# The product of attention's values and factors moves to the end of its period, in front of the split of x

## The chip, the cores and the metric

The kernel runs on one core of one Trainium2 chip. The metric is the device time of one execution in microseconds (us). Engines are named as in the profile: PE (TensorE, matrix products), DVE (VectorE), ACT (ScalarE), POOL (GpSimd) and SP (SyncE, which issues the loads).

## What is computed

Attention with a window of 128 keys and four sink keys, followed by a PReLU network and a mixture of four ReLU experts, all on 1536 tokens of 512 values:

```python
scores = scale * np.matmul(q, k.transpose(0, 1, 3, 2))     # 2 batches, 8 heads, 768 tokens, 64 wide
scores = np.where(is_sink | in_window, scores, -1e9)
a = np.exp(scores - np.max(scores, axis=-1, keepdims=True))
a = a / (np.sum(a, axis=-1, keepdims=True) + 1e-09)
x = np.matmul(a, v)                                         # heads side by side: 1536 x 512
h = x @ w_in                                                # 512 to 2048
x = (np.maximum(h, 0) + alpha * np.minimum(h, 0)) @ w_out   # 2048 to 512
p = domain_probs / (domain_probs.sum(-1, keepdims=True) + 1e-9)
for e in range(4):
    out += p[:, e:e+1] * (np.maximum(x @ w1[e], 0) @ w2[e]) # 512 to 1024 to 512
```

## The kernel before

Each fp32 matrix is split into a high part (rounded to the format that PE multiplies fast) and a low remainder, and a product is three matmuls: high by high, high by low, low by high. Only attention's own products of values and its transposes run on unsplit fp32.

Attention goes through 48 "heads" j of 256 queries (2 batches, 3 blocks of 256 tokens, called units, 8 heads each), one in each **period** p of the loop in `fast`. The work on one head is spread over several periods, so that engines work on different heads at a time. In period p the loop emits, in this order: the split of q and k for head p+2 (`at_split`, ACT); the scores of head p (in periods under 10 of head p+1; `at_scores`, PE); the masking and the row maximum (`at_mask`, DVE, line L587); in odd periods `at_sinks` (PE, L647 and L650); the exponentials (`at_exp`, ACT, L608); in even periods `at_values`, `at_scale` and `at_norm`; the low part of q (`at_split_lo`, DVE, L546); then matmuls of the PReLU network on units that are already through attention (L253 to L255 and L262 to L264), with its PReLU on DVE (`prelu`, L286 and L287) and, where a group of products ends, the copy or addition of its sums (L798, L800); the transposes of the exponentials of head p-1 (`at_turn`, PE L629), and in even periods the split of x (`at_x`: the high part on ACT L698, the low part on POOL L699). At the end, weights are split a piece further (`tick`, L106 to L126). All engines take their instructions in the order in which the program emits them.

Heads are finished in pairs j, j+1 with j even. These are the steps of a pair that matter here:

- period j+2: `at_norm` on DVE makes the reciprocals of the row sums (L617, L618) and copies each to 64 columns (`rw`, L619).
- period j+3: `at_sinks` on PE transposes the sink columns (L647; none for the first unit of a batch) and `rw` (L650) into one PSUM tile `pst`; ACT copies them out (`st` L653, `rb` L655). `rb` are the factors.
- period j+4: `at_values` on PE multiplies values by transposed exponentials into the PSUM tile `pv` (L676); `at_scale` on DVE multiplies `pv` by `rb` into `xf` (L686), the product of this document's title; `at_x` splits `xf`.

So the even period p holds `at_values`, `at_scale` and `at_x` of the pair p-4 and `at_norm` of the pair p-2, and period p+1 holds `at_sinks` of the pair p-2. The tiles `pst` and `pv` share one buffer:

```python
ps = self.psa.tile([P, CH], F32, tag="pv", name=f"pst{j}", bufs=1)   # at_sinks
ps = self.psa.tile([P, CH], F32, tag="pv", name=f"pv{j}", bufs=1)    # at_values
```

The transposes of `at_sinks` in period p+1 can therefore begin only when `at_scale` of period p has read `pv`, and `at_values` of the next pair only when ACT has copied `pst` out. The scores have two buffers. After the 48 heads, `rest` runs the larger part of the PReLU network and the experts.

Of the kernel before, what the change touches and what calls it, by code (L numbers as in the profile page):

```python
# [54 lines left out]
class Body:  # L55
# [661 lines left out]
    def fast(self):  # L717
        nc, tc = self.nc, self.tc
        self.work = accp = tc.alloc_tile_pool(name="accp", bufs=1)
        for c in range(NC):  # L720
            self.acc[c] = accp.tile([P, 4, CH], F32, name=f"acc{c}")
        psb = self.psb = tc.alloc_tile_pool(name="psb", bufs=1, space=PSUM)
        with tc.tile_pool(name="psa", bufs=1, space=PSUM) as self.psa:
            at = self.at = tc.alloc_tile_pool(name="at", bufs=1)
            tmp = tc.alloc_tile_pool(name="tmp", bufs=1)
            self.atk = tc.alloc_tile_pool(name="atk", bufs=1, side="right")
            self.late = []
            for j in range(3, QK):
                self.at_load(j)
            for j in range(2):  # L730
                self.at_split(j)
                self.at_split_lo(j)
            self.plan(*range(EARLY))
            NP, items, before = NU * H, [], None
            for i, visits in enumerate(LEAD):
                steps = [(u, f, f == f0, f == f1 - 1) for u, f0, f1 in visits for f in range(f0, f1)]
                for j, step in enumerate(steps):
                    at_p = LAG + i * H + j * H / len(steps)
                    items.append((at_p, "s1", step))
                    if before:  # L740
                        items.append((at_p + H / len(steps) / 2, "s2", before))
                    before = step
            items.append((NP + 3, "s2", before))
            gs, outs, seen = {}, None, set()
            for p in range(NP + 4):
                if p + 1 >= WHOLE:
                    self.at_load(p + QK + 1)
                self.at_split(p + 2)
                if p in AHEAD:
                    self.busy(psb, 1, f"ahead{p}", tag="h", bufs=2)  # L750
                for j in [0, 1] if p == 0 else [p + 1] if p + 1 < SOON else [] if p < SOON else [p]:
                    self.at_scores(j)
                    if j == 0:
                        self.busy(psb, BETWEEN, "busy", tag="h", bufs=2)
                    if j < WHOLE:
                        self.at_load(j + QK)
                if p > max(LOADS) or p in LOADS:
                    self.load_due(1)
                if FILL.get(p):
                    self.busy(psb, FILL[p], f"busy{p}", tag="h", bufs=2)  # L760
                self.at_mask(p)
                if p == 1:
                    next(self.later_masks)
                if p % 2:
                    self.at_sinks(p - 3)
                self.at_exp(p)
                if p % 2 == 0:
                    self.at_values(p - 4)
                    self.at_scale(p - 4)
                    self.at_norm(p - 2)  # L770
                self.at_split_lo(p + 2)
                if p == 2 * H:
                    self.shares()
                turn = [p - 1]
                while items and items[0][0] < p + 1:
                    _, what, step = items.pop(0)
                    u, f, first, last = step
                    n = slice(u % 2 * UN, (u % 2 + 1) * UN)
                    if what == "s1":
                        ps = psb.tile([P, CH], F32, tag="h", name=f"h{u}_{f}", bufs=2)  # L780
                        self.ready(f)
                        self.s1(f, self.xh[u // 2][:, :, n], self.xl[u // 2][:, :, n], ps[:, :UN])
                        while turn:
                            self.at_turn(turn.pop())
                        gs[step] = self.prelu(tmp, ps[:, :UN], UN, f, f"a{u}_{f}")
                        continue
                    if first:
                        outs = [psb.tile([P, 2, UN], F32, tag="o", name=f"o{u}_{f}_{i}", bufs=2) for i in range(2)]
                    self.s2_transposed(
                        f, *gs.pop(step), [outs[d // 2][:, d % 2, :] for d in range(4)], first, last, [True, False] * 2  # L790
                    )
                    while turn:
                        self.at_turn(turn.pop())
                    if last:
                        for i in range(2):
                            acc = self.acc[u // 2][:, 2 * i:2 * i + 2, n]
                            if u in seen:
                                nc.vector.tensor_tensor(acc, outs[i], acc, ALU.add)  # L798
                            else:
                                nc.vector.tensor_copy(acc, outs[i])  # L800
                        seen.add(u)
                while turn:
                    self.at_turn(turn.pop())
                if p % 2 == 0:
                    self.at_x(p - 4)
                if p == NP + 3:
                    tmp.release()
                    at.release()
                    self.add_late()
                if p < NP + 3:  # L810
                    self.tick(p in STARTS)
                if p == NP - 1:
                    self.atk.release()
                    self.add_late()
                    self.plan(*range(EARLY, SLOTS))
        with tc.tile_pool(name="wide", bufs=1) as wide:
            self.rest(wide, range(len(LEAD), NU), 1)
        psb.release()
        for late in self.late[::-1]:
            late.release()  # L820
        accp.release()
# [232 lines left out]
```

## Time and profile before

| | us |
|---|---|
| median of 3 runs | 896.14 |
| lowest and highest | 894.75, 896.15 |
| the profiled execution, its own time | 895.68 |
| its span in the profile | 893.9 |

The profile is of one execution. Its span runs from the first to the last recorded instruction; what lies around it is 895.68 - 893.9 = 1.78 us. Attention takes the time up to about 207 us, the rest of the networks what follows.

### The profile page before, as it was taken

To read this page: it belongs to the slowest core of one execution; us is meant where nothing else is said; L and a number is where in the kernel's file an instruction comes from. 1 tells how busy PE (TensorE), PEld (TensorE's weight loads), DVE (VectorE), ACT (ScalarE), POOL (GpSimd) and SP (SyncE) were. 2 spreads that over 40 slices of the span, in tenths; PEclk is the share of its full clock that TensorE was granted. 3 is DMA by queue.
4 is the path that set the end of the run, shared out by engine and by line. 5 is a ranking of instruction groups with operands and counts; after the bars stand their busy time and mean duration, and the time that the engine had idled before them with its cause. 6 is when DMAs were issued, how large, how long until landed. Compare 5 with 4: busy or idle time off the path is not lost.

```text
span 893.9 us, 13192 instructions
## 1 busy us (share of the span) xinstructions
PE 881.4 (99%) x4956; PEld 747.4 (84%) x4956; DVE 560.0 (63%) x1104; ACT 330.8 (37%) x773; POOL 368.9 (41%) x349
## 2 busy tenths in 40 slices
PE   9999999999999999999999999999999999999997
PEld 6578899998888888888888888888888888888886
DVE  5778877657995553456655665665566556656654
ACT  4787766754431222233312321231233223212310
POOL 1366644535763454475224404421441344044210
PEclk9999999999999999999999999999999999999999
DMA  5754432302332020000011101101110111011003
GB/s 163 190 184 146 154 120 84 100 1 71 119 118 71 12 70 13 1 25 23 1 48 48 41 7 48 48 3 46 47 48 1 48 48 36 12 48 48 1 1 146
DMA packets 23722, 54.51 MB, mean 61 GB/s; under 512 B 3168, under 2 KB 3168, under 8 KB 23648
## 3 DMA queue, kind: packets, MB, share of 16 engines
q1 hardware_dynamic: 23504, 53.57, 19.0%
q8 instruction: 41, 0.67, 0.3%
q14 instruction: 33, 0.27, 0.1%
q10 hardware_dynamic: 144, 0.00, 0.0%
HBM read 50.42 MB, written 3.15 MB: 60 GB/s over the span
## 4 chain that ended last, share of the span: by engine, by line
PE 93%; DVE 4%; issue 1%; ACT 1%; POOL 0%; DVEq 0%; ACTq 0%; POOLq 0%
PE o L437 9%; PE o L436 9%; PE o L438 9%; PE h L374 5%; PE h L375 5%; PE h L376 5%; PE h L253 5%; PE h L254 5%; PE h L255 5%; PE o L262 5%; PE o L263 5%; PE o L264 5%; PE pv L676 3%; PE c L374 3%; PE c L376 3%; PE c L375 3%
## 5 line engine op out<-in xcount | busy, mean ns | idle before, releaser
L441 DVE SCALAR_TENSOR_TENSOR acc<-o,prob,acc 128x512 f32<-128x512 f32 x180 | 135.1, 751 | 100.3 <-PE o L438 100.3
L140 POOL TENSOR_TENSOR wl<-wraw,wh 128x512 fp32r<-128x512 f32 x60 | 76.6, 1297 | 280.8 <-ACT wh L139 280.8
L437 PE MATMUL o<-wl,hgh 128*128 128x512 f32 x240 | 93.5, 389 | 0.0
L438 PE MATMUL o<-wh,hgl 128*128 128x512 f32 x240 | 93.4, 389 | 0.0
L436 PE MATMUL o<-wh,hgh 128*128 128x512 f32 x240 | 93.4, 389 | 0.0
L253 PE MATMUL h<-xh,wh 128*128 128x256 f32 (+1 forms) x264 | 90.1, 341 | 0.0
L254 PE MATMUL h<-xl,wh 128*128 128x256 f32 (+1 forms) x264 | 87.6, 332 | 0.0
L255 PE MATMUL h<-xh,wl 128*128 128x256 f32 (+1 forms) x264 | 87.4, 331 | 0.0
L289 POOL TENSOR_TENSOR gl<-qk,gh 128x512 fp32r<-128x512 f32 (+1 forms) x36 | 49.5, 1375 | 70.9 <-ACT gh L288 68.7
L288 ACT ACTIVATE gh<-qk 128x512 fp32r<-128x512 f32 (+1 forms) x36 | 21.5, 598 | 122.5 <-DVE qk L287 119.8
L379 DVE TENSOR_TENSOR wraw<-h,wraw 128x512 f32<-128x512 f32 x45 | 31.1, 691 | 48.2 <-PE h L376 46.3
L382 ACT ACTIVATE wraw<-h 128x512 f32<-128x512 f32 x15 | 8.9, 596 | 140.7 <-PE h L376 140.7
L286 DVE TENSOR_SCALAR qk<-h,alpha 128x512 f32<-128x512 f32 (+1 forms) x36 | 25.3, 703 | 53.4 <-PE h L255 53.3
L263 PE MATMUL o<-gl,wh 128*128 128x512 f32 (+1 forms) x144 | 54.0, 375 | 2.5 <-POOL gl L289 2.5
L253 PEld LDWEIGHTS h<-xh,wh 128*128 128x128 f32 x264 | 49.9, 189 | 6.5 <-issue 1.7
L255 PEld LDWEIGHTS h<-xh,wl 128*128 128x128 f32 x264 | 49.9, 189 | 4.8
L254 PEld LDWEIGHTS h<-xl,wh 128*128 128x128 f32 x264 | 50.0, 189 | 4.5
L608 ACT ACTIVATE p<-p,nmax 128x288 f32<-128x288 f32 (+1 forms) x96 | 47.9, 501 | 15.8 <-DVE nmax L587 15.7
L262 PE MATMUL o<-gh,wh 128*128 128x512 f32 (+1 forms) x144 | 53.7, 373 | 0.0
L264 PE MATMUL o<-gh,wl 128*128 128x512 f32 (+1 forms) x144 | 53.4, 371 | 0.0
L438 PEld LDWEIGHTS o<-wh,hgl 128*128 128x128 f32 x240 | 45.0, 188 | 9.4
L436 PEld LDWEIGHTS o<-wh,hgh 128*128 128x128 f32 x240 | 45.0, 188 | 8.9
(209 smaller groups left out, 2440.7 us busy)
## 6 DMA issues: line engine op xcount, KB each, us to landing
wraw<-in_w SPq DMA_DIRECT2D x32, 512.0 KB, 3.6
wraw<-in_w SPq DMA_DIRECT2D x64, 256.0 KB, 2.9
qk<-in_qk SPq DMA_DIRECT2D x21, 352.0 KB, 3.0
v<-in_v SPq DMA_DIRECT2D x12, 256.0 KB, 3.4
out<-acc SPq DMA_DIRECT2D x12, 256.0 KB, 2.3
qk<-in_qk SPq DMA_DIRECT2D x8, 272.0 KB, 3.7
qk<-in_qk SPq DMA_DIRECT2D x11, 176.0 KB, 3.0
qk<-in_qk SPq DMA_DIRECT2D x8, 136.0 KB, 3.4
```

The source lines that it names most:

```text
L140: nc.gpsimd.tensor_tensor(lo, x, hi.bitcast(F32), ALU.subtract)
L253: mm(ps, wh[:, c], xh[:, dk, :], start=dk == 0, stop=False)
L254: mm(ps, wh[:, c], xl[:, dk, :], start=False, stop=False)
L255: mm(ps, wl[:, c], xh[:, dk, :], start=False, stop=dk == DM // P - 1)
L262: mm(outs[dt], wh[:, c], gh, start=first and begins[dt], stop=False, skip_group_check=True)
L263: mm(outs[dt], wh[:, c], gl, start=False, stop=False, skip_group_check=True)
L264: mm(outs[dt], wl[:, c], gh, start=False, stop=last, skip_group_check=True)
L374: mm(ps, bh[:, c], ah[:, d, :], start=first and d == 0, stop=False, skip_group_check=True)
L436: mm(ps, hh[:, n], wh, start=x == 0, stop=False)
L437: mm(ps, hh[:, n], wl, start=False, stop=False)
L438: mm(ps, hl[:, n], wh, start=False, stop=x == 1)
L441: nc.vector.scalar_tensor_tensor(acc, ps, self.prob[:, nt, e:e + 1], acc, ALU.mult, ALU.add)
```

## The change

The line with `at_scale` is taken out from between `at_values` and `at_norm` and put in front of `at_x`, behind the period's network matmuls, its PReLU, its sums and its transposes:

```diff
@@ -766,7 +766,6 @@
                 self.at_exp(p)
                 if p % 2 == 0:
                     self.at_values(p - 4)
-                    self.at_scale(p - 4)
                     self.at_norm(p - 2)
                 self.at_split_lo(p + 2)
                 if p == 2 * H:
@@ -802,6 +801,7 @@
                 while turn:
                     self.at_turn(turn.pop())
                 if p % 2 == 0:
+                    self.at_scale(p - 4)
                     self.at_x(p - 4)
                 if p == NP + 3:
                     tmp.release()
```

No instruction is added or removed, and only `at_scale` changes its place, on DVE. There are 24 of it. What it now stands behind differs by period: the norm alone in periods 12, 14 and 46 (and in 16, with the four short operations of `shares`); the norm and a copy of transposed exponentials (L632) in periods 4 to 10; the norm and L546 in 18, 22, 38 and 42; these and a PReLU (L286, L287) in 20, 24, 30, 32, 36, 40 and 44, in 48 too (without L546); these, with a PReLU or without, and the copy or addition of sums in 26, 28 and 34. In period 50 nothing lies between.

DVE in period 40, before: the product `xf36`, the norm of the pair 38, the low part of q of head 42, a PReLU, and the masking of head 41 (L587), which belongs to period 41. The number behind a name's letters is the head, or unit and block of the network.

```order
L686 TENSOR_TENSOR xf36_2496<-pv36_2485,rb36_2421 128x256
L617 TENSOR_SCALAR den38_2352<-den38_2352 128x4
L618 RECIPROCAL r38_2498<-den38_2352 128x4
L619 COPY rw38_2499<-r38_2498 128x256
L546 TENSOR_TENSOR qs42_2467<-qk2_68,qs42_2467 64x256
L286 TENSOR_SCALAR ga3_4_2527<-h3_4_2505,alpha_77 128x256
L287 SCALAR_TENSOR_TENSOR ga3_4_2527<-h3_4_2505,ga3_4_2527 128x256
L587 ISA p41_2546,nmax41_2547<-s41_0_2540,m23_102 128x288
```

DVE in the same period, of the changed kernel:

```order
L617 TENSOR_SCALAR den38_2352<-den38_2352 128x4
L618 RECIPROCAL r38_2496<-den38_2352 128x4
L619 COPY rw38_2497<-r38_2496 128x256
L546 TENSOR_TENSOR qs42_2467<-qk2_68,qs42_2467 64x256
L286 TENSOR_SCALAR ga3_4_2525<-h3_4_2503,alpha_77 128x256
L287 SCALAR_TENSOR_TENSOR ga3_4_2525<-h3_4_2503,ga3_4_2525 128x256
L686 TENSOR_TENSOR xf36_2530<-pv36_2485,rb36_2421 128x256
L587 ISA p41_2546,nmax41_2547<-s41_0_2540,m23_102 128x288
```

The product went from the front of the norm to behind the PReLU, and still stands ahead of the masking of head 41.

PE at the beginning of period 41, before: the scores of head 41 (L573, L574), the transposes of `at_sinks` for the pair 38, and network matmuls. In brackets stand the engines whose progress an instruction waits for.

```order
L574 MATMUL s41_0_2540<-kl41_2401,qs41_2399 128x288 [waits Pool_49]
L573 MATMUL s41_1_2543<-kh41_2400,qs41_2399 128x288 [waits DVE_49]
L574 MATMUL s41_1_2543<-kl41_2401,qs41_2399 128x288
L647 MATMUL pst38_2550<-ident_81,p38_2348 64x128 [waits DVE_49]
L647 MATMUL pst38_2550<-ident_81,p39_2410 64x128
L650 MATMUL pst38_2550<-ident_81,rw38_2499 128x128 [waits DVE_49]
L650 MATMUL pst38_2550<-ident_81,rw38_2499 128x128
L262 MATMUL o3_0_0_2293<-gha3_3_2447,wh3_802 128x256 [waits Activation_49]
```

PE at the same place of the changed kernel:

```order
L574 MATMUL s41_0_2540<-kl41_2401,qs41_2399 128x288 [waits Pool_49]
L573 MATMUL s41_1_2543<-kh41_2400,qs41_2399 128x288 [waits DVE_49]
L574 MATMUL s41_1_2543<-kl41_2401,qs41_2399 128x288
L647 MATMUL pst38_2550<-ident_81,p38_2348 64x128 [waits DVE_49,PE_49]
L647 MATMUL pst38_2550<-ident_81,p39_2410 64x128
L650 MATMUL pst38_2550<-ident_81,rw38_2497 128x128 x2
L262 MATMUL o3_0_0_2293<-gha3_3_2447,wh3_802 128x256 [waits Activation_49]
```

The order on PE is the same. Before, `pst38` waited for DVE twice: at L647 for the product `xf36`, which frees the buffer, and at L650 for `rw38`. Now one wait at L647, for the product, covers both, since the product comes after `rw38` on DVE.

## Rows read from the trace of the kernel before

**Rows 1.** The page: busy us, share of the span and instructions of each engine.
```profile
PE 881.4 (99%) x4956; PEld 747.4 (84%) x4956; DVE 560.0 (63%) x1104; ACT 330.8 (37%) x773; POOL 368.9 (41%) x349
```

**Rows 2.** Busy time by windows (us from the start), with the clock granted.
```profile
core 0: us, PE busy (x) PEld busy (x) DVE busy (x) ACT busy (x) POOL busy (x), PEclk, DMA share, GB/s
...
12.00:40.00 28.00, 26.79 (x142) 16.36 (x140) 17.50 (x63) 19.42 (x60) 9.67 (x10) 1.00 0.74 206
...
70.00:100.00 30.00, 28.40 (x248) 25.37 (x248) 26.56 (x70) 22.81 (x68) 20.84 (x22) 1.00 0.48 153
100.00:206.00 106.00, 106.00 (x939) 98.25 (x938) 70.85 (x220) 72.47 (x219) 49.24 (x56) 1.00 0.25 78
206.00:230.00 24.00, 21.55 (x163) 20.41 (x162) 20.48 (x35) 10.85 (x23) 14.97 (x14) 1.00 0.30 91
```

**Rows 3.** Who waited for whom, 12 to 206 us: total us, times, longest.
```profile
DVE xf L686 <- PE pv L676: 10.7, 12, 2.6
...
PE pst L650 <- DVE rw L619: 1.8, 4, 0.5
PE s L569 <- DVE nmax L587: 1.1, 2, 0.6
```

**Rows 4.** DVE's lines, 12 to 207 us: the product and the norm's first operation.
```profile
L686 DVE TENSOR_TENSOR xf<-pv,rb 128x256 f32<-128x256 f32 x23 | 9.7, 423 | 17.1 <-PE pv L676 10.7 <-ACT p L608 4.0 <-ACT wh L124 1.8
L617 DVE TENSOR_SCALAR den<-den 128x4 f32<-128x4 f32 x23 | 9.4, 410 | 0.0
```

**Rows 5.** Timeline of period 40 and 41, DVE and PE: start, us, engine, operation.
```profile
167.52 0.48 DVE L286 TENSOR_SCALAR ga<-h,alpha 128x256 f32<-128x256 f32 x1
...
168.03 0.42 DVE L287 SCALAR_TENSOR_TENSOR ga<-h,ga 128x256 f32<-128x256 f32 x1
...
168.21 0.38 PE L647 MATMUL pst<-ident,p 128*64 128x128 f32 x2
...
168.38 0.45 DVE L587 CUSTOM_DVE_ANT_0 p<-s,m 128x288 f32<-128x288 f32 x1
```

**Rows 6.** Timeline of period 48 and 49.
```profile
200.99 0.38 PE L647 MATMUL pst<-ident,p 128*64 128x128 f32 x2
...
201.34 0.42 DVE L287 SCALAR_TENSOR_TENSOR ga<-h,ga 128x256 f32<-128x256 f32 x1
```

**Rows 7.** Timeline of period 28 and 29: the sums' addition.
```profile
115.75 1.41 DVE L798 TENSOR_TENSOR acc<-o,acc 128x512 f32<-128x512 f32 x2
...
116.74 0.38 PE L650 MATMUL pst<-ident,rw 128*128 128x128 f32 x2
```

**Rows 8.** Timeline of period 32 and 33.
```profile
132.45 0.42 DVE L287 SCALAR_TENSOR_TENSOR ga<-h,ga 128x256 f32<-128x256 f32 x1
...
133.96 0.38 PE L650 MATMUL pst<-ident,rw 128*128 128x128 f32 x2
```

**Rows 9.** Timeline of period 18 and 19: PE, ACT and DVE.
```profile
72.27 0.38 PE L647 MATMUL pst<-ident,p 128*64 128x128 f32 x2
73.07 0.44 PE L650 MATMUL pst<-ident,rw 128*128 128x128 f32 x2 [0.42 <-DVE rw L619]
...
72.59 0.40 ACT L698 ACTIVATE xh<-xf 128x256 fp32r<-128x256 f32 x1
...
73.05 0.42 DVE L546 TENSOR_TENSOR qs<-qk,qs 64x256 fp32r<-64x256 f32 x1
...
75.01 1.33 DVE L546 TENSOR_TENSOR qs<-qk,qs 64x256 fp32r<-64x256 f32 x1 [0.66 <-ACT qs L537]
```

**Rows 10.** Timeline of period 20 and 21.
```profile
82.06 0.44 PE L650 MATMUL pst<-ident,rw 128*128 128x128 f32 x2 [0.31 <-DVE rw L619]
...
83.01 0.42 DVE L287 SCALAR_TENSOR_TENSOR ga<-h,ga 128x256 f32<-128x256 f32 x1
```

**Rows 11.** Timeline of period 38: POOL, and DVE's norm.
```profile
157.61 1.16 POOL L547 TENSOR_TENSOR kl<-qk,kh 128x448 fp32r<-128x448 f32 x1
...
157.78 1.01 DVE L617 TENSOR_SCALAR den<-den 128x4 f32<-128x4 f32 x1
```

## The prediction

> **What bounds the kernel now.** I read the page first, then the windows, then the waits by engine, and last the timelines of single periods. The page says that PE is busy 881.4 of 893.9 us [rows 1]: time can go only where PE idles, and whatever makes PE wait is time lost unless PE idles later anyway. The windows say where PE idles during attention [rows 2]: 1.21 us from 12 to 40 us, 1.60 us from 70 to 100 us, and nothing at all from 100 to 206 us, where it is busy 106.00 of 106.00 us. The reader should see two stages. Until about 100 us DVE is as loaded as PE (26.56 of 30 us from 70 to 100). From 100 us on PE alone sets the pace and DVE has a third of its time free (70.85 of 106 us).
>
> The waits name what holds each [rows 3]. DVE stands in front of the product `xf` for 10.7 us in 12 periods, waiting for the product of values on PE; with what else is put in front of it, 17.1 us [rows 4]. That looks like the wait to get rid of, but an idle DVE costs nothing unless PE then waits for it, and PE's own waits in the stage are small: 1.8 us for `rw` (4 times) and 1.1 us for the masking (twice).
>
> **The change part by part.** The number of operations stays the same on every engine, and the product keeps its 423 ns [rows 4]. What changes is who stands behind whom. Three things wait for the product: the high part of x on ACT, the low part on POOL behind that, and the transposes of `at_sinks` in the next period, since `pst` takes the buffer that the product frees. PE executes in order, so all its work waits with them.
>
> *Periods 4 to 12, a gain.* In periods 4 to 8 the norm now runs while DVE would have stood before the product, and DVE comes about a microsecond earlier to the masking (10.7 us in 12 waits, 0.9 us each). That is more than PE's two waits for the masking, 1.1 us together [rows 3], and removes them. I take -1.1 us; bounds 0 (the gain is lost again before 70 us) and -1.6 (one of PE's four waits for `rw`, 0.45 us, goes as well).
>
> *The PE-bound stretch from 100 us, the pairs with a PReLU and nothing else on PE.* Period 40 stands for three (36, 40, 44). Before, the PReLU's second operation starts at 168.03 and DVE's next, the masking of head 41, at 168.38 [rows 5]. The product now takes that place: 168.38 + 0.42 = 168.80. PE goes on at most 0.05 us later (in [rows 9] L650 follows `rw` at 73.07, where DVE's next instruction begins at 73.05). PE came to L647 at 168.21. It waits 168.85 - 168.21 = 0.64 us. The PReLU itself can't come earlier, although the product no longer stands ahead of it: it waits for PE's matmuls, which have not moved. So 3 x 0.64 = 1.9 us.
>
> *Period 48.* There are no more scores, and PE comes to L647 at 200.99, before the PReLU's second operation even starts, at 201.34 [rows 6]. The product starts 0.34 us behind that (the distance of DVE's instructions in rows 5 is 168.38 - 168.03 = 0.35) and ends at 201.34 + 0.35 + 0.42 = 202.11: PE waits 1.2 us.
>
> *Periods 26, 28 and 34, with sums.* In period 28 the two additions occupy DVE from 115.75 to 117.16 [rows 7]; the product then ends about 117.5, PE came to `pst` at 116.74, and waits about 0.8 us. The additions can't come earlier either: the second needs PE's last matmul of the sum. The other two have the same form; I put 0.7 us each. Together 2.2 us.
>
> *Periods with room.* In period 32 the PReLU's second operation starts at 132.45 and PE reaches `pst` only at 133.96, as it has network matmuls in between [rows 8]: the product is done at 133.2 and costs nothing. So in 30. In 46 the product stands behind the norm alone, and in 38 and 42 behind the norm and L546, about where PE comes to `pst`; I take nothing, at most 0.35 us each. What covers these is PE's work between `at_values` and `at_sinks`; without it each would cost up to 0.6 us as in period 40.
>
> The stretch gives 1.9 + 1.2 + 2.2 = 5.3 us; bounds 4.0 (two of the seven waits hidden) and 6.3 (38, 42 and small waits added). It is a sum of waits on an engine without idle time.
>
> *Periods 18 to 24, DVE and PE both loaded.* In period 18 PE stands at `pst` until 73.07 as it is, for `rw` [rows 9]. The product, now behind `rw` and L546 (73.05), starts about 73.4 and ends 73.8 (0.35 us less, if the norm begins earlier by that, which enters the lower bound); L647 (before at 72.27) starts then, and L650 follows at about 74.1, 1.0 us later than before. ACT loses more: it took `xf` at 72.59 and can now do so at 73.85, 1.26 us later, and behind it stand the splits of weights and of q, and DVE waits for that (L546 at 75.01, idle 0.66 us for ACT). So 1.26 us. In period 20 PE comes to L650 at 82.06 [rows 10]; the product is behind the PReLU (83.01 + 0.35 + 0.42 = 83.78), and L650 follows at about 84.0, 2.0 us later. Of this PE gets back waits that it has there already; I put two of the length of those for `rw` (1.8 us in 4, [rows 3]), 0.9 us: 1.1 us are left. Period 24 is of period 40's form, 0.6 us. Together 3.0 us; bounds 0.5 (most of it falls into DVE's and ACT's own waits) and 4.5 (nothing is given back).
>
> *Behind attention* PE idles 24.00 - 21.55 = 2.45 us from 206 to 230 us [rows 2]. DVE, ACT and POOL split weights there behind PReLUs that wait for PE, so I let all of it move along with PE. The loads are all on SP, whose order doesn't change.
>
> **The sum.** -1.1 + 3.0 + 5.3 = +7.2 us, on 895.68 us: 902.9 us, 0.8% more. The median of the runs before is 0.46 us above that execution, less than I can resolve.
>
> **The rivals.** *Faster: DVE's wait is what the time hangs on.* The norm's operations meet POOL: in period 38 the first, `den`, took 1.01 us beside a POOL instruction of 1.16 us that began just before it [rows 11], and its mean is 410 ns [rows 4]. A norm that is moved up may meet POOL idle, and the product behind it may be done before PE comes. Then PE's waits for `rw` and the masking vanish and nothing replaces them: at most the 1.21 + 1.60 = 2.8 us that PE idles from 12 to 40 and from 70 to 100 us [rows 2], 892.9 us. It decides if the product ends before PE reaches `pst`. Against it: the product's end in periods 36, 40, 44 and 48 follows from rows that don't hang on POOL. The Trainium skill has the rule for this rival (SBUF — State Buffer, section "SBUF: two separate sides"): the ports that VectorE and GpSimd share are an exclusive lock, and whichever starts first has them for its whole instruction. By that rule an earlier `den` could win against POOL; the trace agrees as far as `den` ended at 158.79, 0.02 us after POOL's instruction.
>
> *No change:* PE's waits at `pst` do come, but in the first 100 us they fall into waits that are there already, and the early gain and half the late waits cancel: -1.1 + 0.5 + 2.0 = +1.4, 897.1 us. For it speaks that `at_sinks` has waited at this place before; against it, that PE has no idle time from 100 to 206 us which could absorb anything.
>
> *Given back later:* the waits come, but the weights' splits go on meanwhile, and the 2.45 us of idle time from 206 to 230 us shrink to nothing: 902.9 - 2.45 = 900.4 us, still slower. For it: DVE and ACT have free time. Against it: the splits stand in program order behind instructions that wait for PE.
>
> **How the numbers follow.** Chances: all of it moves to the end, as in the sum, 0.58; given back later 0.22; no change 0.10; faster 0.10. About 0.2% (1.8 us) is what a measurement of this kernel can tell from no change. The first two are slower; so slower 0.80, same 0.10, faster 0.10. The range takes the bounds of the terms: low -1.6 + 0.5 + 4.0 = +2.9 less a part of the 2.45, 897.9 us; high 0 + 4.5 + 6.3 = +10.8, 906.5 us. It leaves out the faster case and most of no change.
>
> **What would show it.** In the changed trace PE should stand at L647 or L650 with a wait that ends with `xf` L686: 0.6 us in periods 24, 36, 40 and 44, more in 26, 28, 34 and 48, nothing in 30, 32 and 46; the window of PE's attention work behind 100 us should show some 5 us of idle time. DVE's 10.7 us before the product should be nearly gone. PE's two waits for the masking should be gone, and ACT's `xh` be later in period 18. I am wrong if PE's wait for the product stays below 2 us in total, or if the weights' stage behind attention shortens by as much as attention grows.

## The result and the profile after

The changed kernel takes 907.12 us (median of 4 runs, 906.40 to 907.38) against 895.53 us (4 runs of the kernel before beside them): ratio 1.013, 95% interval 1.0117 to 1.0143, or 11.6 us more. The forecast was 902.9 us, with a range up to 906.5: the direction was right, the size was not.

The page of the changed kernel: span, and busy time by engine, as in [rows 1].

```profile
span 905.2 us, 13180 instructions
...
PE 883.0 (98%) x4956; PEld 748.6 (83%) x4956; DVE 565.7 (63%) x1104; ACT 331.5 (37%) x773; POOL 368.7 (41%) x349
```

PE does the same 4956 matmuls and is busy 1.6 us longer, in a span that is 11.3 us longer: 9.7 us of the loss are idle time of PE. Its windows, to be read against [rows 2]:

```profile
12.00:40.00 28.00, 27.64 (x155) 17.93 (x154) 18.29 (x67) 20.23 (x63) 10.75 (x11) 1.00 0.71 212
40.00:70.00 30.00, 29.38 (x228) 22.64 (x227) 24.26 (x66) 24.29 (x68) 16.98 (x18) 1.00 0.58 175
70.00:100.00 30.00, 24.41 (x202) 22.16 (x203) 22.77 (x56) 21.30 (x61) 17.36 (x19) 0.94 0.38 122
100.00:206.00 106.00, 100.63 (x876) 92.23 (x873) 73.45 (x218) 70.27 (x214) 49.92 (x56) 1.00 0.26 83
217.20:241.20 24.00, 21.58 (x162) 20.28 (x161) 21.06 (x35) 10.71 (x22) 14.49 (x14) 1.00 0.28 90
```

Three things have changed. From 12 to 40 us PE is busy 0.85 us longer than before, the early gain. From 70 to 100 us it idles 5.59 us instead of 1.60, and the granted clock of that window is 0.94 instead of 1.00. From 100 to 206 us it idles 5.37 us where it had not idled at all; the wait of period 24 falls into this window here, that of period 48 behind it. The last window is 206 to 230 us of the kernel before, moved by the 11.2 us that PE is late when attention ends: PE idles 2.42 us there, against 2.45 before. Nothing is given back. PE's waits for the product in the changed kernel (total us, times, longest):

```profile
PE pst L647 <- DVE xf L686: 10.9, 10, 2.7
...
PE pst L650 <- DVE xf L686: 1.8, 3, 0.9
```

DVE's lines of the norm's first operation and of the product in the changed kernel, 12 to 212 us (behind the bar total us, mean ns, and idle time in front of them):

```profile
L617 DVE TENSOR_SCALAR den<-den 128x4 f32<-128x4 f32 x23 | 10.9, 474 | 0.9 <-ACT p L608 0.9
L686 DVE TENSOR_TENSOR xf<-pv,rb 128x256 f32<-128x256 f32 x23 | 9.6, 417 | 0.2
```

DVE no longer stands before the product (0.2 us instead of the 17.1 in [rows 4]); PE stands 10.9 + 1.8 = 12.7 us for the product instead. Its waits for `rw` and the masking [rows 3] are gone. Where the time is lost shows in the timelines of periods 18 to 21, the places of [rows 9, 10]:

```profile
72.28 0.42 ACT L698 ACTIVATE xh<-xf 128x256 fp32r<-128x256 f32 x1 [1.26 <-DVE xf L686]
72.30 0.41 PE L647 MATMUL pst<-ident,p 128*64 128x128 f32 x2 [1.79 <-DVE xf L686]
...
74.73 1.33 DVE L546 TENSOR_TENSOR qs<-qk,qs 64x256 fp32r<-64x256 f32 x1 [1.74 <-ACT qs L537]
...
79.42 1.04 POOL L114 TENSOR_TENSOR wraw<-wraw 128x512 int32<-128x512 int32 x1 [1.09 <-DVE wraw L113]
80.02 0.47 DVE L617 TENSOR_SCALAR den<-den 128x4 f32<-128x4 f32 x1
...
82.71 0.42 DVE L287 SCALAR_TENSOR_TENSOR ga<-h,ga 128x256 f32<-128x256 f32 x1
83.05 0.41 DVE L686 TENSOR_TENSOR xf<-pv,rb 128x256 f32<-128x256 f32 x1
83.61 0.54 PE L647 MATMUL pst<-ident,p 128*64 128x128 f32 x2 [2.67 <-DVE xf L686]
83.95 0.64 PE L650 MATMUL pst<-ident,rw 128*128 128x128 f32 x2
```

PE stands 1.79 us in period 19 and 2.67 us in period 21, each until the product is done. Behind the second wait comes what no step of the prediction had. The windows of the changed kernel there (the granted clock stands third from the end):

```profile
82.00:83.00 1.00, 0.00 (x0) 0.00 (x0) 0.93 (x3) 0.00 (x0) 0.00 (x0) 1.00 0.00 0
83.00:84.00 1.00, 0.39 (x3) 0.41 (x4) 1.00 (x5) 0.83 (x3) 0.34 (x1) 0.85 0.77 200
84.00:85.00 1.00, 1.00 (x6) 1.00 (x5) 0.22 (x2) 1.00 (x3) 1.00 (x2) 0.50 0.21 78
85.00:86.00 1.00, 1.00 (x7) 1.00 (x6) 0.60 (x1) 1.00 (x5) 0.95 (x2) 0.50 0.00 0
86.00:87.00 1.00, 1.00 (x7) 1.00 (x6) 0.73 (x1) 1.00 (x5) 1.00 (x2) 0.50 0.00 0
87.00:88.00 1.00, 1.00 (x10) 1.00 (x9) 0.00 (x0) 0.68 (x3) 0.74 (x1) 0.94 0.48 78
```

TensorE's granted clock is 0.50, that is 1.2 instead of 2.4 GHz, from about 83.7 to 87.1 us, directly behind that idle time: 6 or 7 matmuls end in a microsecond where 10 or 11 do at full clock.

The periods from 26 on look as forecast: waits in 26, 28, 34, 36, 40, 44 and 48, none in 30, 32 and 46. Period 40, the place of [rows 5], and the wait behind period 48:

```profile
176.81 0.41 DVE L686 TENSOR_TENSOR xf<-pv,rb 128x256 f32<-128x256 f32 x1
177.34 0.14 PEld L647 LDWEIGHTS pst<-ident,p 128*64 128x64 f32 x2 [0.77 <-PE s L574]
177.37 0.38 PE L647 MATMUL pst<-ident,p 128*64 128x128 f32 x2 [0.57 <-DVE xf L686]
...
212.21 0.38 PE L647 MATMUL pst<-ident,p 128*64 128x128 f32 x2 [1.09 <-DVE xf L686]
```

### The profile page after: what moved, and what is told of

Same layout as the page of the kernel before. It is cut to its first block, busy times and chain, and to the rows that moved or that the text cites. A ratio compares the mean times of both kernels' runs of the same rounds, so it can differ in the third digit from the quotient of the medians.

```text
span 905.2 us, 13180 instructions
## 1 busy us (share of the span) xinstructions
PE 883.0 (98%) x4956; PEld 748.6 (83%) x4956; DVE 565.7 (63%) x1104; ACT 331.5 (37%) x773; POOL 368.7 (41%) x349
## 4 chain that ended last, share of the span: by engine, by line
PE 93%; DVE 5%; issue 2%; ACT 1%; POOL 0%; DVEq 0%; ACTq 0%; POOLq 0%
PE o L437 9%; PE o L436 9%; PE o L438 9%; PE h L253 5%; PE h L375 5%; PE h L376 5%; PE h L374 5%; PE h L254 5%; PE h L255 5%; PE o L262 5%; PE o L263 5%; PE o L264 5%; PE pv L676 3%; PE c L374 3%; PE c L376 3%; PE c L375 3%
## 5 line engine op out<-in xcount | busy, mean ns | idle before, releaser
L286 DVE TENSOR_SCALAR qk<-h,alpha 128x512 f32<-128x512 f32 (+1 forms) x36 | 25.3, 703 | 53.3 <-PE h L255 53.2
```

## The experiments

**How they are read.** In each profiled execution the start of PE's first L650 in an odd period (p17 is period 17) is compared with that in the kernel before; from each shift that of period 5 is taken off, which is the start of the execution alone (-1.1 to +0.3 us). A difference between two columns is what the periods between them cost, in us. Medians are against the kernel before on the same chip (895.65, 895.74 and 895.37 us; 31, 15 and 21 runs).

| kernel | p17 | p19 | p21 | p23 | p25 | p35 | p49 | median us | ratio, 95% interval |
|---|---|---|---|---|---|---|---|---|---|
| changed kernel | -1.5 | 0.1 | 2.5 | 3.9 | 5.4 | 8.2 | 11.8 | 907.12 | 1.0130 (1.0117 to 1.0143) |
| own_after | -2.5 | -2.0 | -0.6 | -0.6 | 0.0 | 0.1 | 0.5 | 896.01 | 1.0006 (0.9997 to 1.0016) |
| behind_norm | -2.3 | -1.7 | -0.9 | -0.5 | -0.5 | -0.5 | -0.5 | 894.84 | 0.9993 (0.9983 to 1.0002) |
| first_only | -1.5 | -1.1 | -1.1 | -1.1 | -1.1 | -1.0 | -1.1 | 894.08 | 0.9985 (0.9975 to 0.9994) |
| mid_only | 0.0 | 1.1 | 3.6 | 4.8 | 6.3 | 6.3 | 6.3 | 899.95 | 1.0047 (1.0031 to 1.0062) |
| late_only | 0.0 | 0.0 | 0.0 | 0.0 | 0.0 | 2.7 | 6.4 | 901.54 | 1.0065 (1.0050 to 1.0081) |
| fill | -1.5 | 0.1 | 2.6 | 2.5 | 4.0 | 6.8 | 10.5 | 906.07 | 1.0113 (1.0098 to 1.0129) |
| own_tick | -2.5 | -2.0 | -0.3 | -0.3 | -0.3 | -0.3 | 0.1 | 897.33 | 1.0011 (1.0002 to 1.0020) |
| first_mid | -1.5 | 0.1 | 2.6 | 3.7 | 5.2 | 5.2 | 5.2 | 900.63 | 1.0061 (1.0046 to 1.0077) |
| mid_fill | 0.0 | 1.1 | 3.6 | 3.6 | 5.1 | 5.1 | 5.1 | 900.49 | 1.0058 (1.0042 to 1.0073) |
| norm_first | -2.2 | -2.2 | -2.3 | -2.3 | -2.3 | -2.3 | -2.3 | 893.67 | 0.9981 (0.9972 to 0.9990) |
| own_skip_mid | -2.5 | -2.0 | -2.0 | -2.0 | -2.0 | -2.0 | -1.5 | 893.86 | 0.9983 (0.9974 to 0.9992) |

**Is it the buffer? own_after and own_before.** The tile `pst` leaves the buffer of `pv` and goes into the two buffers that the network's `h` tiles use, in the changed kernel (own_after) and in the kernel before (own_before):

```diff
-        ps = self.psa.tile([P, CH], F32, tag="pv", name=f"pst{j}", bufs=1)
+        ps = self.psb.tile([P, CH], F32, tag="h", name=f"pst{j}", bufs=2)
```

> The changed kernel, with the transposes of at_sinks in the buffers of the network's h instead of pv's, so that they no longer need the product to have been read. Theory A (PE waits for the buffer that the product frees, and that is all of the loss): every wait of PE for xf at L647 and L650 is gone, the gain of the first periods stays, and the time is 892.5 to 894.5 us, 1 to 3 below before. Theory B (ACT stands before the late product with the split of x, and everything behind it on ACT is late): PE no longer waits at L647, but the time stays at least 3 us above before, 898 or more.

> The kernel before, with the same other buffer for at_sinks: the control. Both theories: the product is early there, so nothing waits for its buffer; within 1 us of before (895.5).

own_before took 895.36 us (0.9999, 0.9990 to 1.0009): the other buffers alone are worth nothing. own_after took 896.01 us: with the wait for the buffer, 11.1 of the changed kernel's 11.6 us are gone. Its windows:

```profile
70.00:100.00 30.00, 27.16 (x232) 23.55 (x231) 25.18 (x62) 22.43 (x65) 19.10 (x20) 1.00 0.42 128
100.00:206.00 106.00, 105.44 (x928) 97.66 (x928) 74.67 (x220) 71.15 (x216) 49.98 (x57) 1.00 0.26 78
```

PE's waits in own_after that stand at these places:

```profile
PE pst L650 <- DVE rw L619: 2.5, 4, 0.8
...
PE h L254 <- POOL xl L699: 0.6, 2, 0.4
```

No wait for the product and no fall of the clock are left. But the early gain, 2.5 us by period 17, is gone by period 25, so the time missed the 892.5 to 894.5 us that Theory A gave; Theory B's 898 or more did not come either. The buffer explains nearly all of the loss, but not what becomes of the early gain.

**Which position? behind_norm.** The line stands directly behind `at_norm`, with nothing else between:

```diff
                     self.at_values(p - 4)
-                    self.at_scale(p - 4)
                     self.at_norm(p - 2)
+                    self.at_scale(p - 4)
```

> The product moved only behind the norm, not behind L546, the PReLU and the sums. Theory A: the loss comes with what stands between the product and the end of the period, so that the pairs from period 26 on lose nothing, the first keep the gain of 1 to 2 us, and periods 18 to 24 wait up to 0.5 us each for a product behind the norm that POOL holds: 893.5 to 896.5. Theory C (the loss comes from the norm standing in front of the product, by POOL's instructions that hold the norm): at least half of the loss remains, 901 or more.

894.84 us, from the kernel before not to be told apart and in Theory A's range, though three of the waits in periods 18 to 24 are 1.0 to 1.2 us long and not up to 0.5. PE still waits for the product four times (3.7 us in total), all of it before period 25, and is busy 106.00 of 106.00 us from 100 us on. So going behind the norm costs the late periods nothing; what the product stands behind after that (L546, the PReLU, the sums) costs them.

**The change by periods: first_only, mid_only, late_only.** The late position in the periods under 18, in 18 to 24, or from 26 on alone; elsewhere the old one. For mid_only:

```diff
                     self.at_values(p - 4)
+                    if not (18 <= p < 26):
+                        self.at_scale(p - 4)
                     self.at_norm(p - 2)
...
                 if p % 2 == 0:
-                    self.at_scale(p - 4)
+                    if 18 <= p < 26:
+                        self.at_scale(p - 4)
                     self.at_x(p - 4)
```

> The product at the end of its period only in periods 4 to 16, else where it was. From the changed kernel's trace PE is 2.1 us ahead at period 17. Theory A: that lead has nothing to be lost to afterwards, and the time is 893 to 894, 1.5 to 2.5 below before. Theory D (the lead is given back, because DVE and not PE sets the pace in periods 18 to 24): 895 to 896, no change.

> The product at the end of its period in periods 18, 20, 22 and 24 only. In the changed kernel's trace PE falls back by 6.9 us from period 17 to 25, part of which is the lead of 1.5 us that it had there and lost by waiting for the same product. Theory A (each of the four waits at L647 counts in full): 5 to 7 us slower than before, 900.5 to 902.5. Theory E (the prediction's own figure: half of these waits falls into waits that are there already): 3.0 us slower, 898 to 899.5.

> The product at the end of its period from period 26 on only. Theory A (a PE without idle time adds up its waits, 6.5 us from period 25 to 49 in the changed kernel's trace; the prediction had 5.3 less period 24): 901.5 to 902.5. Theory F (what the weights' splits behind attention give back): 899.5 or less.

The early periods alone gain 1.6 us, the middle ones cost 4.2, those from 26 on cost 5.8: 8.4 together, not 11.6. (first_only ended 0.08 us above Theory A's range, mid_only between the ranges of its two theories, late_only in Theory A's.) The traces do add up: by period 49 -1.1 + 6.3 + 6.4 = 11.6, against 11.8 of the changed kernel. The gap lies in mid_only, whose profiled execution took 902.06 us and the other three 899.5 to 900.0. The mean granted clock of that one was 0.997, as in all four of the changed kernel; of the others 0.998 and 0.999.

**What does the clock cost? fill and mid_fill.** Matmuls on constants, with results that nobody reads, are put on PE ahead of the two long waits, in the changed kernel (fill) and in mid_only (mid_fill), so that PE does not idle there:

```diff
+                if p in (19, 21):
+                    self.busy(psb, 7 if p == 21 else 4, f"fill{p}", tag="h", bufs=2)
                 if p % 2:
                     self.at_sinks(p - 3)
```

> The changed kernel, with dummy matmuls on PE ahead of at_sinks in period 19 (4) and 21 (7), where PE stands idle for 1.8 and 2.7 us. The granted clock was 0.50 from 84 to 87 us in the changed kernel's profile, right after the second of these. Theory G (the drop follows PE's idle time and costs PE about half of 3.2 us): with the dummies the clock stays at 1.00 there and the time is 1.2 to 1.8 us lower, 905.3 to 905.9. Theory H (what the clock costs there is hidden behind DVE): the clock stays up, and the time is that of the changed kernel within 0.5 us, 906.6 to 907.6.

> The product stands late in periods 18 to 24 alone, with 4 and 7 matmuls on constants, whose results nobody reads, put in front of the waits at pst in periods 19 and 21. Theory L (what separates the profiled execution of the kernel with periods 18 to 24 alone, 902.06 us, from its other three, 899.5 to 900.0, is the clock's fall behind PE's idle 2.65 us): no execution above 900.4, median 899.6 to 900.2, and the clock at 1.00 from 80 to 92 us. Theory M (the spread has another source): the same spread as there, an execution near 902.

The windows behind the wait of period 21, of fill and then of mid_fill:

```profile
84.00:88.00 4.00, 4.00 (x33) 3.82 (x32) 2.51 (x7) 3.87 (x11) 3.34 (x4) 1.00 0.26 70
...
85.00:86.00 1.00, 1.00 (x10) 1.00 (x9) 0.42 (x4) 1.00 (x3) 1.00 (x2) 1.00 0.51 196
86.00:87.00 1.00, 1.00 (x11) 1.00 (x10) 0.41 (x1) 1.00 (x4) 0.97 (x2) 1.00 0.00 0
```

In both, the clock stays at 1.00, and the step from period 21 to 23 goes from 1.4 to 0.0 us (fill) and from 1.2 to 0.0 (mid_fill); all other steps stay. So in the traces the fall of the clock costs 1.3 us, and the median of fill is 1.05 us below the changed kernel's, between what the two theories gave; against the kernel before on its own chip each is 10.3 and 11.6 us slower, 1.3 us apart. mid_fill has no execution near 902 (899.74 to 900.93), but two above 900.4, and its median is 0.5 us above mid_only's instead of level with it (0.9 us, each against the kernel before on its own chip), outside what was expected. So the medians do not show that the clock alone sets mid_only's 902.06 us apart. What made its three other executions faster than mid_fill stays open: there is no trace of them, and the start alone differs by up to 1.4 us between the profiled executions here.

**Do early gain and middle loss depend on each other? first_mid.** Late in all periods below 26 (`if p < 26` in place of `18 <= p < 26`).

> The product stands late in all periods below 26 and in its old place from 26 on. Theory J (the parts add up once the clock is in the account): the early periods give back 1.5 us, periods 18 to 24 cost 6.3 us with the fall of PE's granted clock and 4.2 without it, so 900.5 us in executions whose clock falls and 898.4 in those where it does not; with the 5.8 us of the periods from 26 on, the first of these is the whole loss of the change. Theory K (PE's lead of 1.5 us makes its waits in 18 to 24 longer by as much, so that the early gain is lost there): 899.9 to 902.0, no better than the kernel with periods 18 to 24 alone.

900.63 us lies in Theory K's range and 0.1 us beside Theory J's 900.5, so the median does not decide. The traces do. The step from 17 to 19 is 1.6 us, 1.1 without the early lead (mid_only); the step from 19 to 21 is 2.5 in both. So 0.5 of the 1.5 us lead is lost in period 18. That is not the late product's doing: first_only, with the product in its old place there, loses as much (-1.5 to -1.1), as PE waits for `rw` longer than the 0.42 us in [rows 9]:

```profile
71.19 0.44 PE L650 MATMUL pst<-ident,rw 128*128 128x128 f32 x2 [0.67 <-DVE rw L619]
```

first_only's -1.1 and mid_only's 6.3 make the 5.2 of first_mid. The two parts do not depend on each other, as Theory J has it, with an early gain of 1.1 us in place of 1.5. With late_only's 5.8 us this kernel's 5.3 give 11.1 of the 11.6 us.

**What is left without the buffer? own_tick and own_skip_mid.** own_tick is own_after with the split of x (`at_x`) of periods 18 to 24 moved behind `tick`, so that ACT no longer holds up the weights' and q's splits for it. own_skip_mid is own_after with the old position of the product in those periods (`if p < 18 or p >= 26` at the late place).

> The kernel with the late product and its own buffer for at_sinks, with the split of x in periods 18 to 24 moved behind the weights' instructions, so that ACT splits weights in place of waiting for the product. Theory B for the rest (with PE free of the buffer, the lost 2.5 us from period 17 to 25 come from ACT's wait of 1.27 us for the product ahead of the split of q, which DVE then waits for): PE loses less than 1.5 us from period 17 to 25, and the time is 0.7 to 1.8 us below that kernel's 896.0, 894.2 to 895.3. Theory I (DVE's own order, product and masking behind the norm, costs these 2.5 us): 895.6 to 896.4, no change.

> The tile pst has two buffers of its own, and the product stands late everywhere except in periods 18 to 24. Theory P (with the buffer gone, what is left of the loss lies in periods 18 to 24, through ACT and POOL, which take x later): the early gain stays, 893.9 to 894.5 us. Theory Q (the rest of the loss is spread over the periods from 26 on too): 895.2 to 896.0.

own_after loses 3.0 us from period 17 to 49, 2.5 of them by period 25. own_skip_mid keeps 2.0 us of the early gain through period 35 and 1.5 to the end, and takes 893.86 us, 0.04 below Theory P's range: 2.0 of the 3.0 us go with the old position in periods 18 to 24. The other 1.0 it loses too, half in period 18, as first_only does, and half in period 36. own_after's trace shows how the late product acts in periods 18 to 20:

```profile
72.02 0.42 ACT L698 ACTIVATE xh<-xf 128x256 fp32r<-128x256 f32 x1 [1.27 <-DVE xf L686]
...
73.30 0.39 PE L254 MATMUL h<-xl,wh 128*128 128x256 f32 x1 [0.43 <-POOL xl L699]
...
74.45 1.34 DVE L546 TENSOR_TENSOR qs<-qk,qs 64x256 fp32r<-64x256 f32 x1 [1.72 <-ACT qs L537]
...
81.49 0.44 PE L650 MATMUL pst<-ident,rw 128*128 128x128 f32 x2 [0.85 <-DVE rw L619]
```

ACT's `xh` stands for the product, POOL's `xl` and ACT's split of q come later, and PE waits for `xl` and, in period 21, for `rw`. In own_skip_mid ACT's wait is gone, L546 stands 0.67 us and PE 0.30 us for `rw`. own_tick missed both ranges. Its trace shows why it gains next to nothing; in period 19

```profile
74.39 0.39 PE L254 MATMUL h<-xl,wh 128*128 128x256 f32 x1 [1.55 <-POOL xl L699]
```

PE waits for the low part of x instead. Its 11 executions fall into two groups, 894.7 to 895.8 and 897.3 to 897.7 us, at mean clocks of 0.999 to 1.0 and 0.997 to 0.998. The trace is of the first; that a fall of the clock makes the second was not seen.

**The gain alone: norm_first.** The product directly behind the norm in periods under 18, in the old place from there on:

```diff
                     self.at_values(p - 4)
-                    self.at_scale(p - 4)
+                    if p >= 18:
+                        self.at_scale(p - 4)
                     self.at_norm(p - 2)
+                    if p < 18:
+                        self.at_scale(p - 4)
```

> The product directly behind the norm in periods 4 to 16, where DVE would otherwise stand before it, and in its old place from 18 on. Theory N (the early gain comes from the norm's going first, and nothing of it needs the product to be last): 893.7 to 894.3 us, as in the kernel with the late place in those periods alone. Theory O (the gain needs the PReLU in front of the product too): 895.0 to 895.7.

893.67 us, 0.03 below Theory N's range: 1.7 us less than the kernel before, about as little as can be told from no change. It is the lowest median here, but first_only (1.6) and own_skip_mid (1.5) gain as much within the noise. PE is busy throughout the first window:

```profile
12.00:40.00 28.00, 28.00 (x159) 18.52 (x158) 20.09 (x70) 20.62 (x63) 10.82 (x11) 1.00 0.72 210
```

The gain is the norm's going first while DVE would stand before the product; moving the product further than that adds nothing that these runs can tell.

## Why the prediction was right in direction and wrong in size

The steps of the table's first row against the prediction's terms, in us:

| term | predicted | measured |
|---|---|---|
| periods 4 to 12 | -1.1 | -1.5 |
| period 18 | 1.26 | 1.6 (1.1 without the early lead, in mid_only) |
| period 20 | 1.1 | 2.4 |
| period 22 | 0 | 1.4, all of it the clock's (0.0 in fill) |
| period 24 | 0.6 | 1.5 |
| periods from 26 on | 5.3 | 6.5 |
| sum | 7.2 | 11.8, less 0.6 at the start: the span's 11.3 |

**The mechanism was right.** PE waits at `pst` until the product has read `pv`, in the periods named; own_after shows that the buffer is what links them. DVE's wait was worth nothing beyond the early gain, as said, and that gain was in its bounds: PE's two waits for the masking are gone.

**The step that failed is the middle term, 3.0 against 6.9 us**, in three places. First, in period 20 the sentence "Of this PE gets back waits that it has there already; I put two of the length of those for `rw`". The 2.0 us were the distance of L650 in the two kernels (82.06 to 84.0), and the wait for `rw` that disappears (0.31 us, [rows 10]) is already inside that distance. It was taken off a second time, and a further one with it, that no row placed there. PE's 2.67 us less 0.31 are the measured 2.4. That is 0.4 more than 2.0, and 0.3 of it is ACT's delay, which the prediction had put into period 18: there PE lost what its own step at `pst` gave (1.0 us worked out, 1.1 in mid_only), while DVE's L546 stood 1.74 us for ACT and came 0.3 us later (74.73, or 75.34 without the 0.6 us of the start, against 75.01), and with it the PReLU and the product of period 20. Second, "Period 24 is of period 40's form, 0.6 us" was not looked up. The timeline of the kernel before has there

```profile
100.08 0.38 PE L647 MATMUL pst<-ident,p 128*64 128x128 f32 x2
...
100.79 0.42 DVE L287 SCALAR_TENSOR_TENSOR ga<-h,ga 128x256 f32<-128x256 f32 x1
```

PE comes to L647 0.71 us before the PReLU's second operation; in period 40 it comes 0.18 us after it [rows 5]. By the prediction's own steps the product ends at 100.79 + 0.35 + 0.42 = 101.56, and PE goes on 1.5 us late, which is what it did. Third, the clock: a wait was priced by its length alone, and the half clock behind it cost 1.3 us more. The upper bound of the term, 4.5 us, contained neither the second nor the third. Of the measured 6.9 us, 0.5 is early lead that period 18 takes back with the product in its old place too (first_only).

**The late term was mis-sized, 6.5 for 5.3**, by a little in each wait: 0.73 us instead of 0.64 in 36, 40 and 44 (PE's matmul begins 0.15 us behind the product's end, 177.22 to 177.37, not 0.05), 1.0, 0.9 and 0.8 in 26, 28 and 34, 1.3 in 48, and 0.2 and 0.1 in 38 and 42, taken as nothing.

**The rivals.** *Given back later* did not happen: in the 24 us of work behind attention PE idles 2.42 us, 2.45 before. *No change* needed the middle waits to fall into others and half the late ones to cancel; they cost 6.9 and 6.5 us. *Faster* had the norm meet POOL less often. It meets it more: `den` takes 474 ns in the mean, 410 before [rows 4], and 15 of the 23 take over 0.3 us, 8 before; each of these ends 0.02 to 0.04 us after an instruction of POOL, and the others take 0.15 to 0.18 us. In period 20 of the kernel before, the product stood beside POOL's L114 and `den` came at the end of that (79.71 + 1.04 = 80.75):

```profile
79.71 1.04 POOL L114 TENSOR_TENSOR wraw<-wraw 128x512 int32<-128x512 int32 x1 [1.09 <-DVE wraw L113]
...
80.30 0.42 DVE L686 TENSOR_TENSOR xf<-pv,rb 128x256 f32<-128x256 f32 x1
...
80.63 0.16 DVE L617 TENSOR_SCALAR den<-den 128x4 f32<-128x4 f32 x1
```

Now `den` stands in the product's place, begins at 80.02 in the midst of L114, and ends at 80.49, 0.03 us after it. So the norm, moved up by the product's 0.33 us, gives 0.31 us of that back. The Trainium skill's rule (SBUF — State Buffer, section "SBUF: two separate sides") is that the shared ports are an exclusive lock, which an instruction of GpSimd, or one of VectorE of certain kinds, has to its end, whichever starts first. It agrees with these rows; it worked against the moved norm, not for it.

## What to carry to other kernels

Before moving an instruction later, ask who needs the buffer that it frees: here all but 1.7 us of DVE's 17 us of standing were free (norm_first), and the engine that set the pace paid for them through one shared PSUM buffer. Where several waits are alike, look up the two rows that set each one, and take a saved wait off only once, since a distance between two positions contains it already. A wait on TensorE of a few microseconds may cost more than its length, if the clock falls behind it; and where one half of a move gains (the norm first, in periods with DVE standing), make that half alone.

## What the hardware showed that was not expected

In the changed kernel, after 1.79 us of idle time ending at 72.30 and 2.67 us ending at 83.61, the granted clock of TensorE was 0.50 for some 3.4 us; after 1.79 us alone it had stayed at 1.00. first_mid's trace has the same fall: 0.86, 0.50, 0.50, 0.50 and 0.93 in the microseconds from 82 to 87. With about the same positions but PE kept busy on constants it stayed at 1.00, and 1.3 us were saved. The product, with one operand in PSUM, took 0.41 to 0.42 us beside POOL's instructions as without them, where the norm's `den` took 0.16 us at the end of one (kernel before, period 20) and 0.47 in the midst of it.
